# Maxima of two key chunks as a + relu(b - a), for some tiles of an attention kernel

## The chip, the cores and the metric

The kernel runs on one core of a Trainium2 chip. The metric is the device time of one execution in microseconds (us); the kernel before takes 2791.81 us, the median of three runs. Two kernels are compared by runs that are taken in turn on the same chip.

The core has five engines with a queue each: TensorE (PE in the profile, with its weight loads as PEld), VectorE (DVE), ScalarE (ACT), GpSimd (POOL), and SyncE (SP), which issues most DMAs. An engine works its queue in order and waits on semaphores of the others. Matrix products go into banks of 128 x 512 fp32 in PSUM; everything else is in SBUF or, for the DMAs' intermediate copies, in DRAM.

## The reference

Two equal layers, each an attention block and a routed feed-forward block, on one sequence of S = 2048 tokens of D = 512. The attention has H = 32 heads of 16 that share one key and one value head.

```python
def _A_ref(x, wq, wk, wv, wo):
    q = (x @ wq).reshape(B, S, 32, 16).transpose(0, 2, 1, 3)
    k, v = x @ wk, x @ wv                      # one head for all
    scores = einsum("bhqd,bkd->bhqk", q, k) * 16 ** -0.5
    o = einsum("bhqk,bkd->bhqd", softmax(scores), v)
    return o.transpose(0, 2, 1, 3).reshape(B, S, 512) @ wo

def _B_ref(x, w_r, w_gate, w_up, w_down):      # two tokens of 2048
    r = x @ w_r
    idx = argsort(-r)[:, :2]
    x_sel = x[idx]
    y = (silu(x_sel @ w_gate) * (x_sel @ w_up)) @ w_down
    return x + scatter(idx, y * sigmoid(r[idx]))

x = x + _A_ref(layernorm(x), ...); x = x + _B_ref(layernorm(x), ...)   # twice
```

The softmax takes the maximum of each row of `scores`, over all 2048 keys, away before the exponential. The change is about how those 2 x 32 x 2048 maxima are found.

## The kernel before

*Tiling.* The keys of a layer lie in `k_st` (128 rows x 2048), the same in the upper and in the lower half of the rows; each half has three groups of 16 rows that take a key's high and low part, so that three products of reduced-precision operands add up to an fp32 product (48 rows), and two rows more for the maximum (50 rows). The queries of a unit `u` lie in `q_st[u]`, again one set in each half. There are NU = 32 units a layer, each with 16 tiles of maxima and KT = 16 steps of scores.

*Maxima.* A tile `mi` stands for 128 queries of a head in each half and two of the four key chunks (CW = 512 keys): even tiles take chunks 0 and 1, odd tiles chunks 2 and 3. Its four products `max_mm(mi, n)` (L391 to L406) are in this order: n = 0 upper half, first chunk; 1 lower half, first chunk; 2 and 3 the same with the second chunk. Each takes one of the four banks `pM`, and VectorE reduces the bank to one column of `mx[u]`: column c by key chunk. `max_parts` (L410) takes the maximum over the four chunks and splits it in two parts on GpSimd; two steps later `max_rows` (L422) turns it on PE, copies it on ScalarE to `mr`, and SP sends it into the two extra rows of `q_st[u]`. From then on the scores of that unit's block come out of the product as score less maximum.

*Scores.* A step `t` has four: `scores(t, i)` (L437), lower half of the rows for even i, upper half for odd i, into one of three banks `pS`; ScalarE's exponential (L455) writes it to `pr`. `pv_mm` (L457) multiplies the exponentials with the values into the one bank `pO`, in four column groups. A column of ones in `v_ext` gives the sums.

*Order.* Every queue's order is written out: the order of the calls is the order of the instructions. The loop at L930 goes over the steps; a tile comes 12 steps ahead of the step with its number (`made`, L375; 8 to 12 at the start of a layer), so the unit's maxima are ready when its scores begin. In a step, each of the four scores is followed by one product of the tile, so that the two lie on different halves of the rows; after every third score (RUN = 3, counted through the steps as 4 t + i) come the pO products that are ready, and after them one step of a piece of projection work (`between`, L496: four products of L187 into a free part of the pO bank): q of a later group, or o of an earlier one, the latter with a copy on ScalarE and a sum on GpSimd. So a run ends after the third score of step 0, the second of step 1, the first and the fourth of step 2, and so on, modulo 3. Other work is put at steps by `at(step, f)`: DMAs of q and of the sums' reciprocals, layer norms on GpSimd, keys and values of the next layer.

*Keys of the next layer.* When the tokens of a chunk have their new values, layer 0 makes the next layer's keys of the chunk at steps `t + 4` (`kv_piece`, products; copies to `kvf` and `kp` on ScalarE and GpSimd), `t + 6` (`k_store`, one DMA, and `kv_v`) and `t + 8` (`k_spread`, six DMAs into `k_sts[1]`). For chunk 1 `t` is 420. The last chunk and the two routed tokens come behind layer 0's last step (L1143 to L1197): the two tokens' keys are made once more (`pk`, `kn`, L1175 to L1188) and put over the two columns of `k_sts[1]`.

*Start of a layer.* Nothing can be scored before unit 0's first block has its maxima. `first` (L925 to L928) gives the order of the first products there: key chunk by key chunk, as the keys arrive. In layer 1 the list is twelve products, four of tile 4, then the rest of the first four tiles.

*Buffers.* `qf` (128 x 128, two buffers) takes q's and o's pieces on their way from pO through GpSimd (L343, L573, L611). `load_wd` (L848) loads w_down in eight parts near the end of a layer into buffers that are free by then, the last four rows into four buffers `wd` of their own.

Of the kernel before, what the change touches and what calls it, by code (L numbers as in the profile page):

```python
# [9 lines left out]
F32 = mybir.dt.float32  # L10
BF = mybir.dt.bfloat16
FR = mybir.dt.float32r
U32 = mybir.dt.uint32
AF = mybir.ActivationFunctionType
OP = mybir.AluOpType
# [30 lines left out]
HALVES = 3  # L46

# [7 lines left out]
def interleaved_layers(ctx, tc, x_in, wq, wkv, wo, w_r, w_gate, w_up, w_down, out):  # L55
# [57 lines left out]
    k_sts = [work.tile([P, S], FR, name="k_st", bufs=2) for _ in range(2)]  # L113

    x2_d = dram.tile([S, D], F32, name="x2_d")
    z_d = [dram.tile([2 * TPC, CW], F32, name=f"z_d{i}") for i in range(2)]
    zr_d = [dram.tile([2 * TPC, CW], F32, name=f"zr_d{i}") for i in range(2)]
    k_d = [dram.tile([P, 2, P], F32, name=f"k_d{i}") for i in range(NCH)]
# [169 lines left out]
    def k_spread(li, c):  # L288

        for i in range(2 * NSLOT):  # L290
            n, h = divmod(i, 2)
            r = h * HR + n * DH
            src = k_d[c].rearrange("(j x) m t -> x m j t", j=TPC)[:DH, n // 2]
            dst = k_sts[li][r:r + DH, c * CW:(c + 1) * CW].bitcast(F32).rearrange("x (j t) -> x j t", j=TPC)
            nc.sync.dma_start(dst, src)

    def kv_v(li, c):
        kf = kvs.pop(c)[0]
        pv = aux([P, TPC, 2 * DH], F32)
        nc.tensor.transpose(pv.rearrange("p j x -> p (j x)"), kf, ident)  # L300
        nc.scalar.copy(v_exts[li][:, c * TPC:(c + 1) * TPC, 1:32:2], pv[:, :, DH:])
# [60 lines left out]
    def layer(li, src_d, dst_d, early=None):  # L362
# [26 lines left out]
        mx, mi = {}, 0  # L389

        def max_mm(mi, n):  # L391
            u, i = divmod(mi, 16)
            if i == 0 and n == 0:
                mx[u] = work.tile([P, 4, 16], F32, name="mx", bufs=3)
            pm = bank()
            nq = cuts[u]

            b, r = divmod(i, 16 // nq)
            x, c = divmod(r, 2)
            j, s = divmod(x, 4 // nq)  # L400
            h, c = 1 - n % 2, 2 * c + n // 2
            q = (b * 4 // nq + s) * P
            r = slice(h * HR, h * HR + KQ)
            nc.tensor.matmul(pm, q_st[u][r, j, q:q + P], k_st[r, c * CW:(c + 1) * CW], start=True, stop=True)  # L404
            i = b * 16 // nq + h * 8 // nq + 2 * s + j
            nc.vector.reduce_max(mx[u][:, c, i:i + 1], pm, axis=AX.X)  # L406
# [388 lines left out]
        for c in range(NCH):  # L795
# [31 lines left out]
            for b in range(TPC):  # L827
# [9 lines left out]
                if li == 0:  # L837
                    t += 4 if c < NCH - 2 else 3
                    at(t, next_x, i, nc.gpsimd)
                    at(t + 2, ln_t, i)  # L840
                    if b == TPC - 1:
                        at(t + 4, whole, kv_piece, c)
                        at(t + 6, k_store, li + 1, c)
                        at(t + 6, kv_v, li + 1, c)
                        at(t + 8, k_spread, li + 1, c)
        wd, wu = [], []

        def load_wd(n):  # L848
# [5 lines left out]
            else:  # L854
                for k in range(2):
                    if n == 3:
                        w = work.tile([P, D], F32, name="so0", bufs=8)
                    elif n < 6:
                        w = work.tile([P, D], F32, name=("qh", "ql")[n - 4])
                    else:  # L860
                        w = work.tile([P, D], F32, name="wd", bufs=4)
# [64 lines left out]
        first[12:12] = [(4, n) for n in range(4)]  # L926
# [3 lines left out]
        for t in range(-LEAD0, last):  # L930
# [4 lines left out]
            mms = [(m, n) for m in tiles for n in range(4)]  # L935
            mms = [first[4 * m + n] if 4 * m + n < len(first) else (m, n) for m, n in mms]
# [230 lines left out]
        for tok in toks:  # L1167
            of = nc.snap(tok // P)
            xb.append((of, work.tile([P, NDC, P], F32, name="xh", bufs=3)))
            nc.gpsimd.tensor_copy(xb[-1][1], xT[:, :, bass.ds(of * P, P)])  # L1170
        q_st.clear()
# [20 lines left out]
        q_stack(0, 0, w, engs=both)  # L1192
        for of, x in xb:
# [42 lines left out]
    in_stats(g4, g4)  # L1236
    kv_v(0, 1)
# [7 lines left out]
    def early():  # L1245
# [3 lines left out]
        kv_v(0, 3)  # L1249
        k_spread(0, 3)  # L1250

# [32 lines left out]
```

## Time and profile before

| What | Value |
|---|---|
| median of three runs | 2791.81 us (2791.6 to 2792.95) |
| the profiled execution | 2793.8 us, its span from first to last instruction 2792.0 |
| mean granted clock of TensorE | 0.985 of full speed |
| busy: PE, VectorE, ScalarE, GpSimd | 2755.8, 2607.0, 2294.5, 720.3 us |
| instructions of PE, VectorE, ScalarE, GpSimd | 39761, 4496, 4705, 1756 |

A busy time is the sum over an engine's instructions of the time in which at least one was in work. PE's matmul ends are modelled, so its 99% says little by itself. A row of the grouped lines reads: line of the kernel, engine, operation, output <- input, shapes, count; then busy us and mean ns of one; then the idle time of the engine just before these instructions, with what ended it. A row of the timeline reads: start in us, length, engine, line, operation, and how many in a row were put together (x). A row of the windows reads: from:to, length, the busy time and count of PE, PEld, VectorE, ScalarE, GpSimd, the granted clock, the DMA engines' share and GB/s.

Layer 0's w_down products begin at 1404.2 us, layer 1's first products for maxima stand at 1424.5 us.

### The profile page before, as it was taken

Reading aid. Unit: us, or ns where it says so; the run is one execution under the profiler, and the core shown is the slowest. Engines: PE = TensorE matmul, PEld = TensorE weight load, DVE = VectorE, ACT = ScalarE, POOL = GpSimd, SP = SyncE. Lnnn points to the kernel's source line nnn. Section 1 sums busy time; section 2 is a strip of 40 time slices with the busy share of each in tenths; the row PEclk is TensorE's granted clock in tenths of the full one; section 3 lists DMA queues with packets and bytes.
Section 4 is the critical chain, followed back from the end, with each engine's and each line's share of the span. In section 5 each row is a group of like instructions: output and inputs, shape, how many; then the busy total and the mean of one; then the engine's idle time right before and its main releaser. Section 6 shows DMA issues by size and latency. Waiting matters only on the chain. (4 is left out here: it accounts for less than half of the span.)

```text
span 2792.0 us, 94326 instructions
## 1 busy us (share of the span) xinstructions
PE 2755.8 (99%) x39761; PEld 1602.5 (57%) x39761; DVE 2607.0 (93%) x4496; ACT 2294.5 (82%) x4705; POOL 720.3 (26%) x1756
## 2 busy tenths in 40 slices
PE   7999999999999999999999999999999999999999
PEld 4655555555555555555656555555555555555555
DVE  7999999999999999999669999999999999999994
ACT  2888888888888888888718888888888888888884
POOL 2100002022451116525510000021124421154262
PEclk8999999999999999999969999999999999999999
DMA  3011110000110001111400000100001100110113
GB/s 110 8 31 34 40 56 18 19 13 19 43 44 18 16 18 48 37 35 42 132 25 9 20 20 20 30 19 16 18 14 51 35 15 20 31 41 22 35 54 122
DMA packets 71386, 97.68 MB, mean 35 GB/s; under 512 B 22732, under 2 KB 32396, under 8 KB 70964
## 3 DMA queue, kind: packets, MB, share of 16 engines
q1 hardware_dynamic: 68098, 89.84, 11.2%
q8 instruction: 313, 5.13, 0.8%
q10 hardware_dynamic: 2354, 1.61, 0.2%
q14 instruction: 109, 0.89, 0.1%
q0 software_dynamic: 512, 0.20, 0.0%
HBM read 43.68 MB, written 17.77 MB: 22 GB/s over the span
## 5 line engine op out<-in xcount | busy, mean ns | idle before, releaser
L406 DVE TENSOR_REDUCE mx<-pM 128x1 f32<-128x512 f32 x4096 | 2508.5, 682 | 84.9 <-PE pM L404 67.5
L455 ACT ACTIVATE pr<-pS 128x512 f32<-128x512 f32 x4044 | 2133.6, 603 | 322.1 <-PE pM L404 232.9
L404 PE MATMUL pM<-k_st,q_st 48*128 48x512 f32 x4096 | 1390.5, 443 | 5.4 <-DVE mx L406 2.4
L453 PE MATMUL pS<-q_st,k_st 50*128 50x512 f32 (+1 forms) x4248 | 1357.2, 422 | 4.6 <-DMA q_st<-mr 2.2
L482 PE MATMUL pO<-pr,v_ext 128*32 128x128 f32 (+1 forms) x22528 | 1175.4, 328 | 2.2 <-ACT so L488 1.9
L453 PEld LDWEIGHTS pS<-q_st,k_st 50*128 50x128 f32 x4248 | 683.1, 186 | 468.4 <-ACT pr L455 265.9
L482 PEld LDWEIGHTS pO<-pr,v_ext 128*32 128x32 f32 x22528 | 562.6, 109 | 527.0 <-issue 347.8
L404 PEld LDWEIGHTS pM<-k_st,q_st 48*128 48x128 f32 x4096 | 669.0, 187 | 33.6 <-DVE mx L406 27.5
L419 POOL CAST mp<-ma 128x8 fp32r<-128x8 f32 (+1 forms) x136 | 26.0, 191 | 834.7 <-PE pM L404 460.9
L613 POOL TENSOR_TENSOR x<-x,qf 128x128 f32<-128x128 f32 x128 | 58.6, 459 | 545.0 <-ACT qf L612 545.0
L187 PE MATMUL pO<-xT,wq_sb 128*32 128x128 f32 x3584 | 180.0, 273 | 0.0
L345 POOL CAST qh<-qf 128x128 fp32r<-128x128 f32 x120 | 34.8, 290 | 513.4 <-ACT qf L344 483.3
L187 PE MATMUL pO<-wo_sb,so 128*32 128x128 f32 x2816 | 137.1, 273 | 0.0
L187 PEld LDWEIGHTS pO<-xT,wq_sb 128*32 128x32 f32 x3584 | 111.3, 110 | 34.0
L634 POOL TENSOR_TENSOR xh<-xh 128x128 f32<-128x128 f32 (+7 forms) x384 | 98.1, 255 | 30.1
L187 PEld LDWEIGHTS pO<-wo_sb,so 128*32 128x32 f32 x2816 | 86.7, 110 | 24.1
L696 POOL TENSOR_TENSOR xh<-xh 128x256 f32<-128x256 f32 (+8 forms) x216 | 66.6, 308 | 15.0
L428 ACT COPY mr<-pM 16x128 f32<-16x128 f32 (+1 forms) x136 | 34.6, 255 | 31.0 <-DVE mx L406 18.0
L346 POOL TENSOR_TENSOR ql<-qf,qh 128x128 fp32r<-128x128 f32 x120 | 55.0, 459 | 9.7
L488 ACT COPY so<-pO 128x256 f32<-128x256 f32 (+1 forms) x136 | 52.6, 387 | 2.1 <-PE pO L482 2.1
L680 POOL TENSOR_SCALAR xh<-x,mv,rs 128x512 f32<-128x512 f32 x24 | 49.9, 2077 | 0.0
L187 PE MATMUL pS<-wo_sb,so 128*32 128x128 f32 (+1 forms) x896 | 44.2, 330 | 0.0
(251 smaller groups left out, 940.5 us busy)
## 6 DMA issues: line engine op xcount, KB each, us to landing
q_st<-qh SPq DMA_DIRECT2D x244, 64.0 KB
q_st<-mr SPq DMA_DIRECT2D x512, 2.0 KB
q_st<-ql SPq DMA_DIRECT2D x122, 64.0 KB
zt<-zr_d SPq DMA_DIRECT2D x120, 64.0 KB
xl_d<-xh SPq DMA_DIRECT2D x28, 256.0 KB
pr<-in_w_up SPq DMA_DIRECT2D x12, 448.0 KB
x<-in_x SPq DMA_DIRECT2D x20, 256.0 KB
x_d<-x SPq DMA_DIRECT2D x16, 256.0 KB
```

Of the source, the lines that this page charges most:

```text
L187: nc.tensor.matmul(out[r], lhsT[:, r], rhs, start=start, stop=stop, skip_group_check=shared)
L346: nc.gpsimd.tensor_tensor(ql, qf, qh.bitcast(F32), op=OP.subtract)
L404: nc.tensor.matmul(pm, q_st[u][r, j, q:q + P], k_st[r, c * CW:(c + 1) * CW], start=True, stop=True)
L406: nc.vector.reduce_max(mx[u][:, c, i:i + 1], pm, axis=AX.X)
L453: nc.tensor.matmul(ps[:, k * 2 * w:(k + 1) * 2 * w], k_st[rows, kt * P:(kt + 1) * P], q_st[u][rows, :, b * w:(b + 1) * w], start=True, sto ...
L455: nc.scalar.activation(pr[hs][:, h, :], ps, AF.Exp)
L482: nc.tensor.matmul(po[u][32 * j:32 * (j + 1), b * w + q.start:b * w + q.stop], v_ext[:, kt, 1 - u % 2:33 - u % 2], p[:, j % 2, k, j // 2, ...
L488: nc.scalar.copy(so[u][:, b * w:(b + 1) * w], po[u][:, b * w:(b + 1) * w])
L613: nc.gpsimd.tensor_tensor(x1[i][:, w], x1[i][:, w], y, op=OP.add)
L634: g.tensor_tensor(t[:, :n], t[:, :n], t[:, n:2 * n], op=OP.add)
L680: eng.tensor_scalar(xl, x1[i], mv2[m][:, b, 0:1], rs2[m][:, b:b + 1], op0=OP.subtract, op1=OP.mult)
L696: nc.gpsimd.tensor_tensor(rp_t[i][:, :n], rp_t[i][:, :n], rp_t[i][:, n:2 * n], op=OP.add)
```

## The change

For a pair of key chunks a and b, max(max a, max b) over positions is the maximum of a + relu(b - a), taken position by position. So the two reductions of a half become three operations: a product with the difference of the keys (chunk 1 less chunk 0), whose bank ScalarE turns by Relu into `over` (128 x 512, SBUF, two buffers); the product with chunk 0; and on VectorE one `tensor_tensor_reduce` that adds `over` to that bank and takes the maximum along the row. The number of products stays. The column of `mx` for chunk 1 is set to -3e38 by GpSimd.

`pairs(mi)` says how many halves of a tile do this: none for odd tiles; both for even tiles below PAIRED (16 in layer 1, 0 in layer 0); else one, the upper half, for tiles with mi % 6 == 2 from 16 on, except in the last unit. The order of a tile's products becomes n = 2, 1, 3, 0 with one pair (upper half's difference; lower half's two chunks; upper half's first chunk, with the sum) or 2, 3, 0, 1 with two (both differences, both sums).

The difference of the keys is made once per layer, from the fp32 values of the two chunks (`kvf`): `k_dif` subtracts on GpSimd into a buffer of `qf`; `k_dif_parts` splits it in high and low part on GpSimd into a buffer of `kp`; `k_dif_store` and `k_dif_spread` send it by one and six DMAs of SP into `k_difs`. In layer 0 this lies among the work ahead of the first step; for layer 1 at steps 425, 428, 429 and 431 of layer 0. For the routed tokens, whose keys change last, the columns of the difference are made anew at the start of layer 1: `xd` subtracts the token's normed activations from those of the token 512 further on GpSimd, `pd` multiplies with the key weights on PE, `kdf`, `kdn` and `k_lo` split, and two copies on GpSimd put the columns into `k_difs[1]`.

At the start of layer 1, `first` holds the products of tiles 1 and 3 in the old order, then those of tile 4, then tiles 0 and 2 with two pairs each. The buffers `wd` give way: the last four rows of w_down go to `over` (two), `so0` (one) and `k_dif` (one).

```diff
--- before
+++ after
@@ -45,6 +45,9 @@
+PAIR = 6
+PAIRED = 0, 16
+
 T_Q, D_Q, T_ST = 2, 3, (13, 29)
@@ -111,10 +114,12 @@
     k_sts = [work.tile([P, S], FR, name="k_st", bufs=2) for _ in range(2)]
+    k_difs = [work.tile([P, CW], FR, name="k_dif", bufs=2) for _ in range(2)]
...
     zr_d = [dram.tile([2 * TPC, CW], F32, name=f"zr_d{i}") for i in range(2)]
+    kd_d = dram.tile([P, 2, P], F32, name="kd_d")
     k_d = [dram.tile([P, 2, P], F32, name=f"k_d{i}") for i in range(NCH)]
@@ -285,17 +290,41 @@
-    def k_spread(li, c):
+    def spread(of, dst):
...
             r = h * HR + n * DH
-            src = k_d[c].rearrange("(j x) m t -> x m j t", j=TPC)[:DH, n // 2]
-            dst = k_sts[li][r:r + DH, c * CW:(c + 1) * CW].bitcast(F32).rearrange("x (j t) -> x j t", j=TPC)
-            nc.sync.dma_start(dst, src)
+            src = of.rearrange("(j x) m t -> x m j t", j=TPC)[:DH, n // 2]
+            nc.sync.dma_start(dst[r:r + DH].bitcast(F32).rearrange("x (j t) -> x j t", j=TPC), src)
+
+    def k_spread(li, c):
+        spread(k_d[c], k_sts[li][:, c * CW:(c + 1) * CW])
+
+    dif = []
+
+    def k_dif():
+
+        d = work.tile([P, P], F32, name="qf")
+        nc.gpsimd.tensor_tensor(d, kvs[1][0], dif.pop(), op=OP.subtract)
+        dif.append(d)
+
+    def k_dif_parts():
+        kf = dif.pop()
+        dif.append(work.tile([P, 2, P], FR, name="kp", bufs=1))
+        nc.gpsimd.tensor_copy(dif[0][:, 0, :], kf)
+        nc.gpsimd.tensor_tensor(dif[0][:, 1, :], kf, dif[0][:, 0, :].bitcast(F32), op=OP.subtract)
+
+    def k_dif_store():
+        nc.sync.dma_start(kd_d, dif.pop().bitcast(F32))
+
+    def k_dif_spread(li):
+        spread(kd_d, k_difs[li])
...
         kf = kvs.pop(c)[0]
+        if c == 0:
+            dif.append(kf)
         pv = aux([P, TPC, 2 * DH], F32)
@@ -386,24 +415,48 @@
-        mx, mi = {}, 0
-
-        def max_mm(mi, n):
-            u, i = divmod(mi, 16)
-            if i == 0 and n == 0:
-                mx[u] = work.tile([P, 4, 16], F32, name="mx", bufs=3)
-            pm = bank()
+        mx, mi, over = {}, 0, {}
+
+        def pairs(mi):
+
+            c = mi % 2
+            if c:
+                return 0
+            if mi < PAIRED[li]:
+                return 2
+            return int(mi >= 16 and mi % PAIR == 2 and mi < 16 * (NU - 1))
+
+        def column(u, i, n):
+
             nq = cuts[u]
-
             b, r = divmod(i, 16 // nq)
...
             h, c = 1 - n % 2, 2 * c + n // 2
-            q = (b * 4 // nq + s) * P
+            return h, c, j, (b * 4 // nq + s) * P, b * 16 // nq + h * 8 // nq + 2 * s + j
+
+        def max_mm(mi, n):
+            u, i = divmod(mi, 16)
+            if u not in mx:
+                mx[u] = work.tile([P, 4, 16], F32, name="mx", bufs=3)
+                for m in range(16):
+                    for half in range(pairs(16 * u + m)):
+                        j = column(u, m, half)[-1]
+                        nc.gpsimd.memset(mx[u][:, 1, j:j + 1], -3.0e38)
+            pm = bank()
+            h, c, j, q, i = column(u, i, n)
+            two = c < 2 and h >= 2 - pairs(mi)
             r = slice(h * HR, h * HR + KQ)
-            nc.tensor.matmul(pm, q_st[u][r, j, q:q + P], k_st[r, c * CW:(c + 1) * CW], start=True, stop=True)
-            i = b * 16 // nq + h * 8 // nq + 2 * s + j
-            nc.vector.reduce_max(mx[u][:, c, i:i + 1], pm, axis=AX.X)
+            k = k_difs[li][r] if two and c else k_st[r, c * CW:(c + 1) * CW]
+            nc.tensor.matmul(pm, q_st[u][r, j, q:q + P], k, start=True, stop=True)
+            if two and c:
+                over[mi, h] = work.tile([P, CW], F32, name="over", bufs=2)
+                nc.scalar.activation(over[mi, h], pm, AF.Relu)
+            elif two:
+                o = over.pop((mi, h))
+                nc.vector.tensor_tensor_reduce(o, pm, o, 1.0, -3.0e38, OP.add, OP.max, mx[u][:, 0, i:i + 1])
+            else:
+                nc.vector.reduce_max(mx[u][:, c, i:i + 1], pm, axis=AX.X)
@@ -843,6 +896,11 @@
                         at(t + 8, k_spread, li + 1, c)
+                        if c == 1:
+                            at(t + 5, k_dif)
+                            at(t + 8, k_dif_parts)
+                            at(t + 9, k_dif_store)
+                            at(t + 11, k_dif_spread, li + 1)
         wd, wu = [], []
@@ -853,12 +911,14 @@
                 for k in range(2):
-                    if n == 3:
+                    if n == 3 or n == 7 and k == 0:
                         w = work.tile([P, D], F32, name="so0", bufs=8)
...
                         w = work.tile([P, D], F32, name=("qh", "ql")[n - 4])
+                    elif n == 6:
+                        w = work.tile([P, D], F32, name="over", bufs=2)
                     else:
-                        w = work.tile([P, D], F32, name="wd", bufs=4)
+                        w = work.tile([P, D], F32, name="k_dif", bufs=2)
                     nc.sync.dma_start(w[:FS], rows[:, k, :])
@@ -923,7 +983,8 @@
         first = [(2 * j + c // 2, c % 2 * 2 + h) for c in range(NCH) for j in range(2) for h in range(2)]
-        first[12:12] = [(4, n) for n in range(4)]
+        late = [(2 * j, n) for j in range(2) for n in (2, 3, 0, 1)]
+        first = [f for f in first if f not in late] + [(4, 2), (4, 3), (4, 0), (4, 1)] + late
         if li == 0:
@@ -932,8 +993,9 @@
                 mi += 1
-            mms = [(m, n) for m in tiles for n in range(4)]
-            mms = [first[4 * m + n] if 4 * m + n < len(first) else (m, n) for m, n in mms]
+            mms = [(m, n) for m in tiles for n in ((0, 1, 2, 3), (2, 1, 3, 0), (2, 3, 0, 1))[pairs(m)]]
+            done = 4 * mi - len(mms)
+            mms = [first[done + k] if done + k < len(first) else f for k, f in enumerate(mms)]
             for i in range(4):
@@ -1168,6 +1230,10 @@
             nc.gpsimd.tensor_copy(xb[-1][1], xT[:, :, bass.ds(of * P, P)])
+        xd = work.tile([P, NDC, 2], F32, name="xd", bufs=1)
+        cols = [nc.snap(tok % CW) for tok in toks]
+        for k, col in enumerate(cols):
+            nc.gpsimd.tensor_tensor(xd[:, :, k:k + 1], xT[:, :, bass.ds(col + CW, 1)], xT[:, :, bass.ds(col, 1)], op=OP.subtract)
         q_st.clear()
@@ -1190,6 +1256,15 @@
         q_stack(0, 0, w, engs=both)
+        pd = aux([P, 2], F32)
+        for k in range(NDC):
+            nc.tensor.matmul(pd, wkv_sb[:, k, :], xd[:, k, :], start=k == 0, stop=k == NDC - 1)
+        kdf, kdn = work.tile([P, 2], F32, name="kdf", bufs=1), work.tile([P, 2], FR, name="kdn", bufs=1)
+        nc.scalar.copy(kdf, pd)
+        nc.gpsimd.tensor_copy(kdn, kdf)
+        k_lo(kdn, kdf, nc.gpsimd)
+        for k, col in enumerate(cols):
+            nc.gpsimd.tensor_copy(k_difs[li + 1][:, bass.ds(col, 1)], kdn[:, k:k + 1])
         for of, x in xb:
@@ -1234,6 +1309,7 @@
     in_stats(g4, g4)
+    k_dif()
     kv_v(0, 1)
@@ -1247,7 +1323,10 @@
         kv_v(0, 3)
+        k_dif_parts()
         k_spread(0, 3)
+        k_dif_store()
+        k_dif_spread(0)
```

## The prediction

> **What bounds the kernel now.** The page's costliest groups name the row that the change is aimed at: 4096 maxima over a 128x512 bank, 2508.5 us of VectorE. The windows view then tells the stretches apart.
>
> ```profile
> L406 DVE TENSOR_REDUCE mx<-pM 128x1 f32<-128x512 f32 x4096 | 2508.5, 682 | 84.9 <-PE pM L404 67.5
> ```
> ```profile
> 100.00:440.00 340.00, 339.55 (x4770) 190.41 (x4762) 335.91 (x575) 299.72 (x607) 28.85 (x81) 1.00 0.13 36
> ...
> 1425.00:1457.00 32.00, 30.43 (x113) 15.19 (x112) 29.50 (x51) 4.48 (x9) 0.78 (x4) 0.55 0.08 20
> 1457.00:1810.00 353.00, 352.46 (x5043) 204.78 (x5041) 346.74 (x592) 306.73 (x621) 27.45 (x82) 0.99 0.08 19
> ```
>
> The busy columns are PE, PEld, DVE, ACT, POOL. VectorE is 99% busy from 100 to 440 us (335.9 of 340) and 98% from 1457 to 1810; elsewhere less, 97% between 1900 and 2100 (193.6 of 200, below). ScalarE has 12 to 13% spare. So in some 693 us (340 + 353) VectorE looks like the bound, elsewhere it does not. PE's own busy says nothing, since its ends are modelled; its starts have to be read. The timeline of PE alone, for some three "runs" (three scores, each beside one product for a maximum, then the pO products):
>
> ```profile
> 302.10 0.50 PE L453 MATMUL pS<-q_st,k_st 50*128 50x512 f32 x1
> ...
> 303.79 0.50 PE L453 MATMUL pS<-q_st,k_st 50*128 50x512 f32 x1
> 303.79 0.72 PE L404 MATMUL pM<-k_st,q_st 48*128 48x512 f32 x2
> 304.12 0.63 PE L453 MATMUL pS<-q_st,k_st 50*128 50x512 f32 x2
> 304.36 0.40 PE L404 MATMUL pM<-k_st,q_st 48*128 48x512 f32 x1
> 304.69 0.86 PE L482 MATMUL pO<-pr,v_ext 128*32 128x128 f32 x16
> 305.36 0.40 PE L187 MATMUL pO<-xT,wq_sb 128*32 128x128 f32 x8
> 305.69 0.50 PE L453 MATMUL pS<-q_st,k_st 50*128 50x512 f32 x1
> ```
>
> A score and its neighbour start together (303.79), on different halves of the rows; the third pair starts 0.24 us after the second (304.36 - 304.12) and 0.57 us into the run. A run without projection takes 1.69 us (302.10 to 303.79), one with eight instructions of it 1.90 us (to 305.69). The grouped lines by form, from 200 to 400 us and (second fence) from 1900 to 2100, say how many there are of each:
>
> ```profile
> L453 PEld LDWEIGHTS pS<-q_st,k_st 50*128 50x128 f32 x327 | 53.2, 185 | 40.3 <-ACT pr L455 26.8 <-issue 9.4
> L404 PEld LDWEIGHTS pM<-k_st,q_st 48*128 48x128 f32 x326 | 52.6, 184 | 0.9 <-DVE mx L406 0.8
> ...
> L187 PE MATMUL pO<-xT,wq_sb 128*32 128x128 f32 x328 | 16.5, 273 | 0.0
> ```
> ```profile
> L406 DVE TENSOR_REDUCE mx<-pM 128x1 f32<-128x512 f32 x315 | 193.6, 682 | 5.5 <-PE pM L404 4.4
> ...
> L187 PE MATMUL pO<-xT,wq_sb 128*32 128x128 f32 x320 | 16.1, 273 | 0.0
> L187 PE MATMUL pO<-wo_sb,so 128*32 128x128 f32 x304 | 14.7, 273 | 0.0
> ```
>
> First stretch: 109 runs (327/3), 41 of them filled (328/8), so 68 x 1.69 + 41 x 1.90 = 192.8 us of 200. Second: 105 runs, 78 filled (624/8): 27 x 1.69 + 78 x 1.90 = 193.8. **PE's undisturbed runs make up all but 7.2 us of the stretch in which VectorE is full, and all but 6.2 us of the other.** The rests hold transposes, block ends and waits; their difference, about 1.0 us in 200, is what a full VectorE costs PE beyond that. The waits agree: weight loads for maxima wait 0.8 us for VectorE, those for scores 26.8 us for ScalarE. The two engines are balanced, and the one whose lateness PE feels is ScalarE.
>
> **The change part by part.** The products `max_mm` issues keep their number. A pair turns two reductions into one relu on ScalarE and one sum with a maximum on VectorE. The rule in `pairs` gives tiles 20, 26 ... 494, 80 per layer with one pair each, and 16 pairs in unit 0 of layer 1: 176.
>
> *VectorE.* Neither view shows a sum-and-maximum with accumulator from a bank and SBUF. Nearest rows:
>
> ```profile
> L998 DVE SCALAR_TENSOR_TENSOR x<-pS,x 128x512 f32<-128x512 f32 x2 | 1.4, 692 | 7.5 <-PE pS L187 7.5
> ...
> L685 DVE DVE_READ_ACCUMULATOR zt<-xh,wr_sb 128x1 f32 x6 | 0.5, 84 | 0.0
> ```
> ```profile
> 1430.05 9.65 DVE L406 TENSOR_REDUCE mx<-pM 128x1 f32<-128x512 f32 x16
> ```
>
> Sixteen reductions in a row take 9.65 us, so a slot is (9.65 - 0.68)/15 = 0.60 us. The new operation by its rows overlaps its neighbour likewise, 0.62 us, plus the accumulator read and its issue, 0.10: 0.72. A pair frees 1.20 - 0.72 = 0.48 us; 176 make 84 us of VectorE. Bounds: 0.60 freed (no read) and below nothing, -0.2, were it two passes of 0.69. I take 0.48.
>
> *What PE gets of it.* Where VectorE is full, 1.0 us per 200 over 693 us: 3.5 us; where it isn't, next to nothing. Bounds: 0, and the whole saving of the pairs there. A step is four scores, 327 of them in 200 us, so 2.45 us, and 693/2.45/6 = 47 pairs x 0.48 = 23 us; that would need the rest of 7.2 us to be VectorE's as well. I take -4.
>
> *ScalarE.* Its timeline:
>
> ```profile
> 302.63 3.26 ACT L455 ACTIVATE pr<-pS 128x512 f32<-128x512 f32 x6 [0.17 <-PE pM L404]
> 306.23 1.58 ACT L455 ACTIVATE pr<-pS 128x512 f32<-128x512 f32 x3 [0.34 <-PE pM L404]
> ```
>
> Three exponentials in 1.58 us: slots of (1.58 - 0.60)/2 = 0.49, 1.47 per run. Spare: 0.22 in an empty run, 0.43 in a filled one. I price the relu as an exponential, 0.49. The single pairs lie in steps with t % 6 == 2 (tile less 12), where a run ends after the first score: the difference's product closes one run, the relu falls between its third exponential and the next run's first. An empty run leaves 0.27 us of it over, and the third score of the run after needs the bank of the third exponential before. That one ends 0.53 (302.63 - 302.10) + 2 x 0.49 + 0.60 = 2.11 us into its run, the third pair of the next run wants it at 1.69 + 0.57 = 2.26: 0.15 of room, less the load and the semaphore. After two empty runs PE stalls about 0.2 us, otherwise about 0.03. By the shares of empty runs (0.62 and 0.26) two come together 0.38 and 0.07 of the time: 0.1 us per pair in the first kind of stretch, 0.04 in the other. 47 x 0.1 + 113 x 0.04 = 9 us. Bounds: 0, and 0.27 at each of 160, 43 us.
>
> [...]
>
> *The difference's making, once per layer.* In layer 0 its DMAs go out while SP is otherwise waiting, before the first pair: nothing. For layer 1, `k_dif` takes one of two `qf` buffers in step 425 and `k_dif_parts` gives it back in step 428, on GpSimd behind `var_pool` and `z_mul`. There the timelines of ScalarE and GpSimd have
>
> ```profile
> 1163.09 0.28 ACT L344 ACTIVATE qf<-pO 128x128 f32<-128x128 f32 x1
> ```
> ```profile
> 1165.25 1.29 POOL L563 TENSOR_TENSOR so<-so,zt 128x512 f32<-128x512 f32 x1
> 1166.49 0.29 POOL L345 CAST qh<-qf 128x128 fp32r<-128x128 f32 x1
> 1166.86 0.46 POOL L346 TENSOR_TENSOR ql<-qf,qh 128x128 fp32r<-128x128 f32 x1
> ```
>
> The write of `qf` at 1163.09 is the second allocation after the difference's, so it must wait for GpSimd: 1165.25 + 1.29 + 0.29 + 0.46 (the last two rows as prices of the copy and the subtraction) = 1167.3. Queued behind it on ScalarE are the exponentials, and PE for their banks. 4.2 us less the spare of a run: +3.8. Bounds 0 (another buffer) and 4.7. SP's new store waits for the same and holds the `mr` rows behind it, inside that time. The 176 memsets on GpSimd run steps before `max_parts` reads them.
>
> *Start of layer 1.* PE's timeline there:
>
> ```profile
> 1417.34 1.87 PE L1177 MATMUL pM<-xn,wkv_sb 128*128 128x2 f32 x8
> ...
> 1420.99 3.60 PE L1196 MATMUL pS<-wkv_sb,xh 128*128 128x16 f32 x16
> 1424.52 1.22 PE L404 MATMUL pM<-k_st,q_st 48*128 48x512 f32 x4
> ```
>
> `pd` is a second group like L1177 (1.87 us), put ahead of L1196, behind which the first maxima stand at 1424.52: +1.9. The rest of it (copies on ScalarE and GpSimd, `k_difs` patched) is covered by the eight maxima that come first, 8 x 0.60. From 1430 to 1457 ScalarE is idle (4.48 of 32 us) and VectorE sets the pace; 12 of the 48 maxima ahead of the first score drop out: 12 x 0.48 = 5.8, less 0.8 for banks that wait for a relu: -5. Together -3; bounds -8 (also the four later pairs, and `pd` hidden) and +2.
>
> *End of a layer.* w_down's last rows move to `over`, `k_dif` and `so0`, whose last readers are done 20 steps before: nothing.
>
> *The sum:* -4 + 9 + 3.8 - 3 = +5.8, against the profiled execution's 2793.8 (span 2792.0). On the median of 2791.81 that is 2797.6; as the 9 counts stalls that partly fall on waits already there, I take 1.6 off: **2796**.
>
> **The rivals.**
>
> *PE's order.* In a tile with one pair the last run holds, lower and upper half of the rows: score up, maximum low; score low, maximum low; score up, maximum up. Each half has three products, but if starts keep the program's order, the upper score waits for the lower maximum and the run grows by one slot of 0.24: 160 x 0.24 = 38 us, 2834. What the trace shows, in the block form where a score is two products on one half:
>
> ```profile
> 1464.29 0.38 PE L453 MATMUL pS<-q_st,k_st 50*128 50x256 f32 x1
> 1464.30 0.50 PE L404 MATMUL pM<-k_st,q_st 48*128 48x512 f32 x1
> 1464.51 0.28 PE L453 MATMUL pS<-q_st,k_st 50*128 50x256 f32 x1
> ```
>
> Both score products are emitted before the maximum's, yet that starts at 1464.30, 0.21 us before the second of them: the halves go on by themselves. Chance 0.11. [...]
>
> *ScalarE has no room.* The stall falls on most pairs, some 0.15 us each instead of 0.06: 160 x 0.15 = 24 us in place of 9, 2811; or the sum takes two passes, which comes near it. It decides where PE's loads for scores wait more than the 26.8 us in 200. This is the slower side's main case: chance 0.16.
>
> *VectorE does set the pace.* If the rest of 7.2 us in the full stretches is mostly VectorE's (block ends wait for maxima rows), the 47 pairs give about 22: -22 - 5 + 13 = -14, 2778. For it: 99% busy. Against: runs of one kind are equally long in both stretches' sums, and only 0.8 us of waits name it. Chance 0.33.
>
> **How the numbers follow.** The forecast has 0.40, with a range of its own of 2789 to 2803. A measurement can tell about 0.2% (5.6 us) from no change. Faster: 0.30 (nearly all of the third rival); same: 0.29 (0.26 of the forecast); slower: 0.41 (0.14 forecast, 0.16, 0.11). The range 2768 to 2814 reaches in the third rival to nearly all that VectorE can give (-23 - 8 + 3.8: 2765), and leaves out PE's order and the ends.
>
> **What would show it.** Steps right: VectorE's busy falls by about 84 us, ScalarE's rises by about 100 (176 relus near 0.60), and the waits of score loads for ScalarE grow; runs with a pair keep their third pair 0.57 us in; a gap of about 4 us on ScalarE at the `qf` write of L344 near 1163. Wrong: runs with a pair 0.24 longer (order), or full stretches that shorten by over 1% (pace).

## The result, and where the profile after differs

The changed kernel takes 2823.97 us (median of four, 2820.69 to 2824.68) against 2792.28 on the same chip: a ratio of 1.0113, 95% interval 1.0100 to 1.0126. It is 1.1% slower, above the range of the prediction (2768 to 2814). Its profiled execution takes 2820.69 us, span 2818.9, clock 0.986.

The page's costliest groups after the change (columns as in the prediction; L459 was L406, L506 was L453, L451 was L404):

```profile
L459 DVE TENSOR_REDUCE mx<-pM 128x1 f32<-128x512 f32 x3744 | 2320.0, 682 | 173.2 <-PE pM L451 138.8
...
L506 PEld LDWEIGHTS pS<-q_st,k_st 50*128 50x128 f32 x4248 | 675.7, 186 | 459.8 <-ACT pr L508 264.2
...
L457 DVE CUSTOM_DVE_ANT_0 over<-pM,over 128x512 f32<-128x512 f32 x176 | 119.5, 682 | 10.7 <-ACT over L454 6.1
L454 ACT ACTIVATE over<-pM 128x512 f32<-128x512 f32 x176 | 110.7, 630 | 10.0 <-PE pM L451 5.4
```

The score loads' row of the page before:

```profile
L453 PEld LDWEIGHTS pS<-q_st,k_st 50*128 50x128 f32 x4248 | 683.1, 186 | 468.4 <-ACT pr L455 265.9
```

The windows of the two stretches that were full of VectorE:

```profile
100.00:440.00 340.00, 339.35 (x4654) 189.92 (x4647) 324.97 (x567) 303.75 (x622) 28.12 (x100) 1.00 0.13 36
```
```profile
1457.00:1810.00 353.00, 351.91 (x4845) 205.87 (x4848) 329.32 (x583) 306.41 (x627) 26.43 (x103) 0.97 0.07 19
```

VectorE has the relief it was to have: 325.0 of 340 us instead of 335.9, over the span 2531.1 instead of 2607.0. The time went up all the same, and the list of idle times does not say where: the score loads' wait for ScalarE is 264.2 us, before 265.9.

Two kernels with one order of scores can be laid side by side. The 136 copies of `pO` to `so`, one at each block's end, show *when* the loss comes:

| Copy | before, us | after, us | difference |
|---|---|---|---|
| first of layer 0 | 81.0 | 78.9 | -2.1 |
| last of layer 0 | 1382.9 | 1395.2 | +12.4 |
| first of layer 1 | 1471.5 | 1483.9 | +12.4 |
| last of layer 1 | 2761.1 | 2787.2 | +26.1 |

The difference grows by 0.24 us from block to block on the mean, through both layers up to the last unit, and by nothing at layer 1's start or near 1163 us. From -2.1 (ahead of any pair; other kernels here stand between -2.9 and +0.8 there) it rises by 28.2 us, 0.18 for each of the 160 single pairs. The *runs* laid side by side (start of a run to start of the next) show where: from 152 to 387 us the 17 runs that hold the sum are 0.184 us longer on the mean, from 1961 to 2617 us 42 such runs 0.116; runs with the difference are unchanged (0.001). Besides, the second run after the sum's is longer by 0.15 to 0.31 in one of four pairs. (By their place among the steps of a block the pairs are of four kinds, mi % 24 = 2, 8, 14 and 20, with 40 pairs each.)

One stalled run, PE's timeline, then its weight loads and ScalarE (after):

```profile
2008.02 0.49 PE L506 MATMUL pS<-q_st,k_st 50*128 50x512 f32 x1
2008.03 0.49 PE L451 MATMUL pM<-k_st,q_st 48*128 48x512 f32 x1
2008.36 0.64 PE L506 MATMUL pS<-q_st,k_st 50*128 50x512 f32 x2
2008.60 0.64 PE L451 MATMUL pM<-k_st,q_st 48*128 48x512 f32 x2
2009.17 0.86 PE L535 MATMUL pO<-pr,v_ext 128*32 128x128 f32 x16
```
```profile
2008.13 0.19 PEld L506 LDWEIGHTS pS<-q_st,k_st 50*128 50x128 f32 x1
2008.36 0.19 PEld L451 LDWEIGHTS pM<-k_st,q_st 48*128 48x128 f32 x1
2008.50 0.18 PEld L506 LDWEIGHTS pS<-q_st,k_st 50*128 50x128 f32 x1
2008.61 0.19 PEld L451 LDWEIGHTS pM<-k_st,q_st 48*128 48x128 f32 x1
```
```profile
2006.88 1.57 ACT L508 ACTIVATE pr<-pS 128x512 f32<-128x512 f32 x3 [0.32 <-PE pM L451]
2008.33 0.62 ACT L454 ACTIVATE over<-pM 128x512 f32<-128x512 f32 x1
```

The third score's weights load at 2008.50, right behind the third exponential of the run before (2006.88 + 1.57 = 2008.45), whose bank it takes. The sum's product is next on the same half of the rows; its weights load 0.11 later, and the pO products start 1.15 us into the run. No idle time is written down for the third score's wait, because the load at 2008.36 covers it: that is why the list of waits shows nothing. A run with a pair that does not stall:

```profile
1977.49 0.50 PE L506 MATMUL pS<-q_st,k_st 50*128 50x512 f32 x1
1977.50 0.50 PE L451 MATMUL pM<-k_st,q_st 48*128 48x512 f32 x1
1977.83 0.41 PE L506 MATMUL pS<-q_st,k_st 50*128 50x512 f32 x2
1978.07 0.41 PE L451 MATMUL pM<-k_st,q_st 48*128 48x512 f32 x2
1978.41 0.86 PE L535 MATMUL pO<-pr,v_ext 128*32 128x128 f32 x16
```
```profile
1974.93 2.76 ACT L508 ACTIVATE pr<-pS 128x512 f32<-128x512 f32 x5
```

Here the exponential is done at 1977.69, 0.20 into the run; both scores start together 0.34 into it, on different halves, both products 0.24 later, and pO follows 0.92 into the run. So the third score now **wants its bank 0.34 into the run, not 0.57**: in the order 2, 1, 3, 0 it is the second product on its half, no longer the third.

The pair whose run follows a transposition has two waits of its own. Weight loads and ScalarE of after near 223 us:

```profile
223.79 0.18 PEld L451 LDWEIGHTS pM<-k_st,q_st 48*128 48x128 f32 x1 [0.21 <-ACT over L454]
```
```profile
223.13 0.62 ACT L454 ACTIVATE over<-pM 128x512 f32<-128x512 f32 x1
```

In a single pair the sum's product is the third behind the difference's; the transposition of the maxima lies in between and takes a bank too, so here the sum's is the fourth. With four banks it comes round, by count, to the difference's, and it waits for the relu (223.13 + 0.62 = 223.75). And the copy of the maxima rows stands behind the relu; ScalarE and SP, then PE, of after and (second set) of before at the same place:

```profile
1992.75 0.62 ACT L454 ACTIVATE over<-pM 128x512 f32<-128x512 f32 x1
1993.22 0.24 ACT L481 COPY mr<-pM 16x128 f32<-16x128 f32 x1
```
```profile
1993.49 2.67 SPq L485 DMA_DIRECT2D q_st<-mr  x4
```
```profile
1992.67 0.28 PE L479 MATMUL pM<-ident,mp 128*16 128x128 f32 x1
...
1996.54 0.50 PE L506 MATMUL pS<-q_st,k_st 50*128 50x512 f32 x1
1996.55 0.73 PE L451 MATMUL pM<-k_st,q_st 48*128 48x512 f32 x2
1996.89 0.86 PE L506 MATMUL pS<-q_st,k_st 50*128 50x512 f32 x2
1997.28 0.50 PE L451 MATMUL pM<-k_st,q_st 48*128 48x512 f32 x1
```
```profile
1973.94 0.25 ACT L428 COPY mr<-pM 16x128 f32<-16x128 f32 x1
```
```profile
1974.22 2.67 SPq L432 DMA_DIRECT2D q_st<-mr  x4
```
```profile
1973.63 0.28 PE L426 MATMUL pM<-ident,mp 128*16 128x128 f32 x1
...
1977.52 0.50 PE L453 MATMUL pS<-q_st,k_st 50*128 50x512 f32 x1
...
1978.10 0.46 PE L404 MATMUL pM<-k_st,q_st 48*128 48x512 f32 x1
```

From transposition to copy it is 0.55 us after (1993.22 - 1992.67) and was 0.31 (1973.94 - 1973.63), so SP's sending of the four rows comes 0.23 us later than it did; the third pair of the block's first run, which needs the last of them, starts 0.74 into its run (1997.28 - 1996.54) and started 0.58 into it before.

### The profile page after: what moved, and what is told of

The parts are those of the page before. It is cut to its first block, busy times and chain, and to the rows that moved or that the text cites. A ratio compares the mean times of both kernels' runs of the same rounds, so it can differ in the third digit from the quotient of the medians.

```text
span 2818.9 us, 94876 instructions
## 1 busy us (share of the span) xinstructions
PE 2779.4 (99%) x39769; PEld 1623.4 (58%) x39769; DVE 2531.1 (90%) x4496; ACT 2359.4 (84%) x4882; POOL 732.2 (26%) x1945
## 5 line engine op out<-in xcount | busy, mean ns | idle before, releaser
L459 DVE TENSOR_REDUCE mx<-pM 128x1 f32<-128x512 f32 x3744 | 2320.0, 682 | 173.2 <-PE pM L451 138.8
L506 PE MATMUL pS<-q_st,k_st 50*128 50x512 f32 (+1 forms) x4248 | 1346.5, 425 | 5.2 <-DMA q_st<-mr 1.2
L451 PE MATMUL pM<-k_st,q_st 48*128 48x512 f32 x3920 | 1346.6, 443 | 4.6 <-DVE mx L459 1.5
L506 PEld LDWEIGHTS pS<-q_st,k_st 50*128 50x128 f32 x4248 | 675.7, 186 | 459.8 <-ACT pr L508 264.2
L451 PEld LDWEIGHTS pM<-k_st,q_st 48*128 48x128 f32 x3920 | 637.7, 187 | 34.4 <-DVE mx L459 16.3
L457 DVE CUSTOM_DVE_ANT_0 over<-pM,over 128x512 f32<-128x512 f32 x176 | 119.5, 682 | 10.7 <-ACT over L454 6.1
L454 ACT ACTIVATE over<-pM 128x512 f32<-128x512 f32 x176 | 110.7, 630 | 10.0 <-PE pM L451 5.4
L451 PE MATMUL pM<-k_dif,q_st 48*128 48x512 f32 x176 | 77.5, 451 | 2.1 <-ACT over L454 1.4
```

The lines of the kernel that those rows point to most:

```text
L451: nc.tensor.matmul(pm, q_st[u][r, j, q:q + P], k, start=True, stop=True)
L454: nc.scalar.activation(over[mi, h], pm, AF.Relu)
L457: nc.vector.tensor_tensor_reduce(o, pm, o, 1.0, -3.0e38, OP.add, OP.max, mx[u][:, 0, i:i + 1])
L506: nc.tensor.matmul(ps[:, k * 2 * w:(k + 1) * 2 * w], k_st[rows, kt * P:(kt + 1) * P], q_st[u][rows, :, b * w:(b + 1) * w], start=True, sto ...
```

## The experiments

Theories. **Halves**: the order 2, 1, 3, 0 makes the third score early for its bank. **Bank and rows**: behind a transposition the relu holds a bank and the rows. **ScalarE has no room**: the relu's time stalls PE wherever it stands. **PE's order**: starts keep the program's order, which costs a slot of 0.24 us at each of the 160 pairs. **VectorE sets the pace**, or costs PE the 1.0 us in 200 of the forecast. All kernels are edits of the changed one but `before_rows`; each ran in turn with the kernel before.

**starts_only**: no single pairs (no tile has mi % 1 == 2).

```diff
-PAIR = 6
+PAIR = 1
```

> The change with none of its 160 single pairs (PAIR = 1, so that no tile has mi % 1 == 2); the 16 pairs of layer 1's start and the making of the difference stay. Run by run, the changed kernel's trace shows its loss in the run that holds the sum, 0.18 us on the mean where a run has no projection work and 0.12 where it has, and in one later run of three blocks. If the single pairs are the whole loss (some 29 us by the trace), this takes 2790 to 2797 us. If the loss sits in what is done once per layer (the difference's making, the start), it stays over 2810.

2794.61 us, ratio to before 1.0006 (0.9996 to 1.0015). The single pairs are the whole loss. The 16 pairs at layer 1's start and the making of the difference together are within the measurement of nothing.

**order_alone**: no pair, the order kept.

```diff
-PAIR = 6
+PAIR = 1
...
-            mms = [... ((0, 1, 2, 3), (2, 1, 3, 0), (2, 3, 0, 1))[pairs(m)]]
+            mms = [... ((0, 1, 2, 3), (2, 1, 3, 0), (2, 3, 0, 1))[pairs(m) or int(16 <= m < 16 * (NU - 1) and m % 6 == 2)]]
```

> As starts_only, with the order 2, 1, 3, 0 for the tiles that had a single pair, but plain maxima of all four products: no relu, no sum, no difference there. 'Halves': the third score is still too early for its bank in two of four phases, though no relu runs: 14 to 20 us above starts_only. 'ScalarE has no room': within 3 us of starts_only. 'PE's order': 38 us above starts_only in all phases alike.

2811.57 us, 1.0068 (1.0051 to 1.0085), 17.0 above starts_only. Run by run against starts_only, two of every four such runs are 0.22 to 0.25 longer, the other two unchanged. PE, weight loads and ScalarE of one of them:

```profile
2000.83 0.50 PE L506 MATMUL pS<-q_st,k_st 50*128 50x512 f32 x1
2000.84 0.50 PE L451 MATMUL pM<-k_st,q_st 48*128 48x512 f32 x1
2001.17 0.63 PE L506 MATMUL pS<-q_st,k_st 50*128 50x512 f32 x2
2001.40 0.63 PE L451 MATMUL pM<-k_st,q_st 48*128 48x512 f32 x2
2001.96 0.86 PE L535 MATMUL pO<-pr,v_ext 128*32 128x128 f32 x16
```
```profile
2001.30 0.18 PEld L506 LDWEIGHTS pS<-q_st,k_st 50*128 50x128 f32 x1
```
```profile
1999.67 3.27 ACT L508 ACTIVATE pr<-pS 128x512 f32<-128x512 f32 x6 [0.34 <-PE pM L451]
```

No relu runs, and the run has the stalled one's form: weights at 2001.30, behind the third exponential (1999.67 + 2 x 0.49 + 0.60 = 2001.25), pO 1.13 into the run. Halves holds for this part; PE's order, which would stall all four alike, falls. In the two unchanged kinds something lies between the run before and the sum's run and gives the exponential time: a block's end, with projection products in 38 of 40 (mi % 24 == 20), or a transposition (mi % 24 == 2).

**halves_in_turn**: the pair in an order that keeps the halves apart.

```diff
-((0, 1, 2, 3), (2, 1, 3, 0), (2, 3, 0, 1))
+((0, 1, 2, 3), (2, 1, 0, 3), (2, 3, 0, 1))
```

> The changed kernel with the products of a single pair in the order 2, 1, 0, 3 instead of 2, 1, 3, 0: score and product lie on different halves of the rows all through the run, and the sum's product is two banks behind the difference's, not three. Theory 'halves': with 2, 1, 3, 0 the third score is the second product on its half, 0.24 us earlier than before, when the exponential that frees its bank is not done; the stalls of about 0.23 us in the two of four phases with nothing else in the way go, 80 x 0.22 = 18 us: 2803 to 2809. Theory 'ScalarE has no room': the relu's time on ScalarE is what stalls, wherever the products stand: 2820 to 2828 as with the change. Theory 'PE's order' (one slot of 0.24 for each of 160): 38 us less, about 2786.

2812.97 us, 1.0071 (1.0054 to 1.0088): 11 less than the change, not the 18 that were expected. Where runs have projection work (1961 to 2617 us) the sum's run is unchanged (0.005 over starts_only). Where they have none, the stall has moved to the run behind. Its weight loads and ScalarE:

```profile
302.97 0.18 PEld L506 LDWEIGHTS pS<-q_st,k_st 50*128 50x128 f32 x1 [0.30 <-ACT pr L508]
```
```profile
300.83 0.62 ACT L454 ACTIVATE over<-pM 128x512 f32<-128x512 f32 x1
301.31 2.10 ACT L508 ACTIVATE pr<-pS 128x512 f32<-128x512 f32 x4
```

The third exponential behind the relu ends a slot ahead of the fourth, at 301.31 + 2.10 - 0.49 = 302.92, and the next run's third score waits for it: 0.25 us in two of four such runs. This is the stall that the prediction described: in these places ScalarE has no room for a relu. Over the trace, the runs behind a sum hold 9 us of the loss against starts_only, and the transpositions, which this order leaves as they were, 10.

**beside_rows** and **free_phase**: a fourth of the pairs each.

```diff
-            return int(mi >= 16 and mi % PAIR == 2 and mi < 16 * (NU - 1))
+            return int(mi >= 16 and mi % 24 == 2 and mi < 16 * (NU - 1))
```

and the same with `mi % 24 == 20`.

> The changed kernel with a fourth of its single pairs: only the tiles with mi % 24 == 2, whose sum's run comes right behind the transposition of maxima (step 6 of 8). There the transposition takes a bank between the difference's and the sum's, so the sum's product waits for the relu, and the copy of the maxima rows stands behind the relu, so the next block's first score waits. 'Bank and rows': 40 pairs at 0.24 to 0.46 us, 9 to 18 us above starts_only, about 13. 'ScalarE has no room' shared alike by all pairs: 7 us above starts_only. 'Halves' alone (no stall in this phase but by the order): at most 7.

> The changed kernel with the other fourth of its single pairs, tiles with mi % 24 == 20 (sum's run at the start of a block of 8 steps), where the changed kernel's trace shows no stall in any of the runs (the run before the sum's has projection work). 'Halves' and 'ScalarE': 2793 to 2796, as starts_only. 'PE's order': 40 x 0.24 = 10 us above. If every pair costs alike: 7 us above.

2803.96 us, 1.0044 (1.0030 to 1.0058), and 2793.79, 1.0008 (0.9998 to 1.0018): 9.4 above starts_only and 0.8 below it. The pairs beside a transposition cost 0.24 us each, those of free_phase nothing. In beside_rows, the sum's runs without projection work are 0.265 longer (the bank) and the block's first run 0.19 (the rows); with projection work only the latter is there, 0.235. With order_alone's 17.0 the parts add up to 17.0 + 9.4 - 0.8 = 25.6 of the 29.4 us between the medians of the change and starts_only; their two profiled executions, on which the runs were measured, are 25.6 apart. There the parts are found again, kind by kind: in the change the sum's runs with mi % 24 == 8 and 14 are 17.2 us longer than in starts_only (order_alone: 17.1), those at a transposition 3.0 (beside_rows: 3.2), and the blocks' first runs behind it 7.3 (7.1).

**rows_on_vector**: beside_rows, with the rows' copy on VectorE.

```diff
-            nc.scalar.copy(mr[:2 * n], pt[:2 * n])
+            nc.vector.tensor_copy(mr[:2 * n], pt[:2 * n])
```

> beside_rows (2804.0, 40 single pairs, each with the copy of the maxima rows behind the relu on ScalarE) with all copies of the maxima rows on VectorE in place of ScalarE. 'Rows behind the relu': the stall of the next block's first score, about 0.2 us, goes, 40 x 0.2 = 8 us less: 2795 to 2797. If the whole of beside_rows' loss is the bank of the transposition or ScalarE's time in general: 2802 to 2806.

2808.03 us, 1.0059 (1.0041 to 1.0077): a miss in the time, 4 above beside_rows. At the pairs the stall of the block's first run did fall, from 0.235 to 0.07; but in other blocks, where ScalarE had copied at once, the copy now stands behind maxima on VectorE, and their first runs grew by 0.15 to 0.57. The copy's place behind the relu is confirmed; moving it for every block costs more.

**relief_alone**: VectorE relieved, ScalarE not loaded (on starts_only): 160 maxima leave out 448 of their 512 keys.

```diff
-                nc.vector.reduce_max(mx[u][:, c, i:i + 1], pm, axis=AX.X)
+                few_keys = n == 0 and 16 <= mi < 16 * (NU - 1) and mi % 6 == 2
+                nc.vector.reduce_max(mx[u][:, c, i:i + 1], pm[:, :64] if few_keys else pm, axis=AX.X)
```

> starts_only (2794.6) with VectorE relieved and nothing put on ScalarE: in the 160 halves that had a single pair, the first product's maximum is taken over 64 of its 512 keys, so the computation leaves 448 keys out of those maxima. That frees about 0.45 us of VectorE each, as much as a pair was priced at. 'VectorE sets the pace' where it is 98 to 99% busy: 47 of them at 0.45, 15 to 22 us less than starts_only, 2772 to 2780. 'VectorE costs PE 1.0 us in 200' (the forecast's term): 3 to 4 us less. 'PE and ScalarE set the pace': within 2 us of starts_only.

```profile
L460 DVE TENSOR_REDUCE mx<-pM 128x1 f32<-128x64 f32 x160 | 34.4, 215 | 0.0
```

2794.51 us, 1.0009 (0.9999 to 1.0018), equal to starts_only. VectorE's busy falls from 2598.5 to 2543.0 us, 0.35 for each and not 0.45; were it the pace in the full stretches, 47 x 0.35 = 16 us would show. They don't: **VectorE 99% busy is not the bound**, and its relief is worth nothing here.

**relu_alone** and **relu_of_weights**: 160 relus beside starts_only, of the first product's bank, then of weights in SBUF.

```diff
                 nc.vector.reduce_max(mx[u][:, c, i:i + 1], pm, axis=AX.X)
+                if n == 0 and 16 <= mi < 16 * (NU - 1) and mi % 6 == 2:
+                    nc.scalar.activation(work.tile([P, CW], F32, name="over", bufs=2), pm, AF.Relu)
```

with `wq_sb[:, 0, :]` in place of `pm` in the second.

> starts_only (2794.6) with 160 relus more on ScalarE and nothing else: for the tiles that had a single pair, after the usual maximum of the first product, ScalarE also turns that bank into a buffer that nobody reads. Order of the products, maxima and keys are those of before. In halves_in_turn the stalls stand in the run after the sum's, where the third score waits for the exponential that the relu pushed back, 0.25 us in runs without projection. 'ScalarE has no room there': 10 to 18 us above starts_only, as halves_in_turn (18). If the sum on VectorE or the difference's products cause them: within 3 us of starts_only.

> relu_alone came out 96 us slower because ScalarE waited at each relu until VectorE had reduced the same bank, so it priced a wait, not the relu. Here the 160 relus of starts_only (2794.6) read 512 columns of the weights in SBUF, which nobody writes: ScalarE's time alone, with no bank, no order and no sum. 'ScalarE has no room in runs without projection': the third score of the run behind stalls about 0.25 us there and the copy of the maxima rows behind the relu costs about 0.2 in a fourth of the places: 8 to 18 us above starts_only. If a relu that waits for nothing fits in ScalarE's spare: within 4 us of starts_only.

The first took 2890.37 us, 1.0355 (1.0337 to 1.0374), which no theory had. ScalarE's and VectorE's timelines show why it answers another question:

```profile
306.47 0.60 ACT L461 ACTIVATE over<-pM 128x512 f32<-128x512 f32 x1 [0.38 <-DVE mx L459]
```
```profile
304.55 1.89 DVE L459 TENSOR_REDUCE mx<-pM 128x1 f32<-128x512 f32 x3
```

The relu begins where VectorE's maximum of that bank ends (304.55 + 1.89 = 306.44), and the exponentials stand behind it. In the trace all 160 relus wait for one semaphore, which VectorE alone raises, so it is the program that lets the two readers of a bank run one after the other. The second took 2818.75, 1.0090 (1.0073 to 1.0107): 24 above starts_only, more than expected. By runs it is 0.29 in the run behind where there is no projection work, 0.4 at a transposition, and 0.06 to 0.3 with projection work; over the trace 10 us lie behind the pairs' runs and 12 at transpositions. There this relu holds no bank, and yet the same run stalls: its last product waits for the copy of the rows, which stands behind the relu (its weights load at 225.19, after 0.34 us of idle time; the copy ends at 225.15). ScalarE's time alone is thus dear in the places where the kernel puts it, though ScalarE is 12% idle in the full stretch (299.68 us busy of 340 in starts_only).

**rows_earlier**, then **before_rows** and **pairs_rows**: the maxima rows one step earlier; on halves_in_turn, on the kernel before, and on halves_in_turn again with unit 0's rows left where they were.

```diff
-            at(e + 2, max_rows, u, b)
+            at(e + 1, max_rows, u, b)
```

and `at(e + (1 if u else 2), max_rows, u, b)` in the other two.

> halves_in_turn (2813.0) with max_rows one step earlier (at e + 1 in place of e + 2), so that no transposition stands between a pair's difference and its sum, and no copy of maxima rows stands behind a relu with a score waiting for it. 'Bank and rows': the stalls of tiles with mi % 24 == 2, 40 at 0.2 to 0.46 us, go: 2797 to 2805, what is left being ScalarE's stalls in runs without projection. If those stalls are ScalarE's time wherever the rows stand: 2811 to 2815.

> The kernel before with max_rows one step earlier, except in a layer's unit 0 (where rows_earlier lost 4.9 us at layer 1's first block against starts_only, by the trace). By the traces of rows_earlier and starts_only the first score of a block waits in the kernel before too, for the maxima rows, about 0.1 us at many blocks; with the rows a step earlier that goes. 'Rows are late before too': 128 blocks, 5 to 10 us less than before, ratio 0.9965 to 0.998. If rows_earlier gained only what its pairs had lost: ratio 0.999 to 1.001.

> rows_earlier (2796.6) with unit 0's rows where they were: all 176 pairs in the order 2, 1, 0, 3, max_rows at e + 1 for units from 1 on. 4.9 us less than rows_earlier by layer 1's start: 2790 to 2793. If VectorE's relief were worth anything with the other waits gone, it would come out below before_rows; by ScalarE's stalls in runs without projection it comes out 5 to 9 us above it.

rows_earlier: 2796.64, 1.0011 (1.0001 to 1.0020), 16.3 less than halves_in_turn: with transpositions out of the pair's way and the rows early, nearly all of the loss is gone. before_rows: 2791.99, 1.0000 (0.9991 to 1.0009): the earlier rows gain nothing by themselves; I had expected 5 to 10 us. pairs_rows: 2795.22, 1.0014 (1.0005 to 1.0023): with all waits but one taken away, the change still does not gain.

The one that is left is ScalarE's: in pairs_rows the runs behind the sums with mi % 24 == 14 are 4.4 us longer than in before_rows. Behind those with mi % 24 == 8 this stall is gone, where the transposition now lies between the sum's run and the next one and gives ScalarE time. Other runs are shorter, so that the runs from the first pair to the last of each layer are 1.2 us shorter in all: less than single executions of one kernel differ by (2790.5 to 2794.8 in before_rows). What makes them shorter was not tried. So a relu costs by its place: what stands behind it on ScalarE, and whether PE has other work there.

## Why the prediction was wrong

*What bounds the kernel.* Right: VectorE's 98 to 99% is not what PE waits for (relief_alone). The term of -4 us was 0, to within some 3 us.

*VectorE's saving.* Nearly right: 2598.5 to 2531.1 us of busy time for 160 pairs (starts_only to the change) is 0.42 each, forecast 0.48.

*ScalarE.* Here the step failed that says "the third pair of the next run wants it at 1.69 + 0.57 = 2.26: 0.15 of room". It looked at the run *behind* the pair. In the pair's own run the order 2, 1, 3, 0 puts the third score second on its half, 0.34 into the run. So a reordering that left the count of products on each half alone took 0.23 us of a bank's slack, and order_alone has 17 us for it with no relu at all. The stall that was described exists (halves_in_turn: 9 us behind the sums), but in the change itself, where the sum's run stalls first, the runs behind the sums are only 0.5 us longer in all.

*What was left out.* The transposition's bank and the rows' copy behind the relu, put at nothing with no reason given: 9.4 us in beside_rows, most of it the rows. The prediction named what stands behind the relu on ScalarE as exponentials only.

So the term of 9 us measures 29 (2823.97 - 2794.61), inside the bounds that it was given (0 to 43) and far from the value taken.

*The hold of `qf`, +3.8.* Wrong, it was 0. ScalarE and GpSimd after:

```profile
1168.28 0.27 ACT L665 COPY qf<-pS 128x128 f32<-128x128 f32 x1 [0.87 <-PE pS L192]
...
1174.01 0.28 ACT L373 ACTIVATE qf<-pO 128x128 f32<-128x128 f32 x1
```
```profile
1176.83 0.28 POOL L315 CAST kp<-qf 128x128 fp32r<-128x128 f32 x1
1177.19 0.46 POOL L316 TENSOR_TENSOR kp<-qf,kp 128x128 fp32r<-128x128 f32 x1
```

The write of `qf` at 1174.01 (1163.09 before) doesn't wait for GpSimd's end of the difference at 1177.65. It is the second write behind the difference's, as I had counted (the first is at 1168.28). But the difference still holds one of the two buffers, so it went into the one that the write at 1168.28 had used: the two buffers are not given out strictly in turn, as the prediction assumed.

*Start of layer 1, -3.* Not resolved: the first exponential of a score comes 45.6 us behind the first w_down product instead of 46.6, but at the first block's end the difference between the kernels is 12.4 us, as at layer 0's end. Over the kernels run here this stretch varies by 3 us.

*The rivals.* "PE's order" had the nearest time (2834) by a wrong mechanism, so that was luck: two scores start together at 1977.83, ahead of the product that the program puts between them (1978.07), and the pairs of free_phase cost nothing. "ScalarE has no room" named an engine that has a part in it and 2811, but 17 of the 29 us come with no relu on ScalarE. The price of a relu, an exponential's slot of 0.49, is right (0.48 from a relu to the next instruction, 1992.75 to 1993.22 above), and says nothing of what stands behind the relu.

*What was to be seen.* VectorE's busy fell by 75.9 (84 forecast); ScalarE's rose by 64.9 (100 forecast), 0.37 for each of 176 relus of 0.63, as relus overlap their neighbours (the one at 1992.75 above the copy behind it by 0.15: 1992.75 + 0.62 - 1993.22); score loads' waits for ScalarE did not grow (264.2, before 265.9), and that sign was the wrong one to name: the late load at 2008.50 above, covered by the load at 2008.36, has no idle time written down.

## What to carry to other kernels

Before an instruction stream is reordered, write down for each moved product on which half of the rows it is first, second or third, and which bank it takes from whom: a place earlier was a deadline earlier here (0.34 us into the run instead of 0.57). Every bank and every small copy that stands between belongs to that list, the ones that other helpers issue too. And test first, by relieving an engine without loading another, whether a 99% busy engine is what the others wait for (here it was not: 2794.51 us with VectorE relieved, 2794.61 without).

## What the runs showed of the hardware

In the run at 1977.49 products on different halves of the rows started out of the order of the program: the product between the second and the third score starts at 1978.07, 0.24 behind both (one row, x2 in 0.41 us from 1977.83). So that an engine works its queue in order does not hold for PE's starts there. The other engines kept it in the trace of before: the starts of VectorE (4474 instructions), ScalarE (4702), GpSimd (1747) and SP (1383 DMAs) stand in the program's order, line by line. Two engines that read the same bank did not do so at once in relu_alone: ScalarE was idle for 0.38 us at the relu shown, and for 68 us over 159 of them. There the program's semaphores kept them apart; what the chip does without them was not tried.
